# One transformer block on one core: side work of the vector engine moved between units, chunks paced wider, five low parts split over two engines

## The chip, the cores and the metric

The kernel runs on one core of a Trainium2 chip. The core has a matrix engine (TensorE, PE in the profile, with its weight loads as PEld), a vector engine (VectorE, DVE), an activation engine (ScalarE, ACT), a general engine (GpSimd, POOL) and a queue that issues the transfers (SyncE, SP). Each runs its own instructions in order; semaphores order them among each other. The metric is the time of one execution on the device, in microseconds (us). The kernel before takes 740.03 us, the median of 3 runs (738.38 to 742.38).

## The reference

The block has a modulation vector, attention with a sliding window, and a feed-forward layer with Mish, for S = 2048 tokens of width D = 448, 16 heads of width 28, a window of 256 and F = 1792:

```python
mod = (_silu(c) @ w_mod).reshape(c.shape[0], 6, 1, -1)
sa, ca, ga, sb, cb, gb = (mod[:, 0], mod[:, 1], mod[:, 2], mod[:, 3], mod[:, 4], mod[:, 5])
h = _layernorm(x, axis=-1) * (1 + ca) + sa
x = x + ga * _A_ref(h, A_wqkv, A_wo)
h = _layernorm(x, axis=-1) * (1 + cb) + sb
x = x + gb * _B_ref(h, B_w1, B_b1, B_w2)
```

`_A_ref` projects to q, k and v, takes scores q k / sqrt(28), masks all but the last 256 keys of each query, takes the softmax and the sum over v, and projects with `wo`. `_B_ref` is `mish(h @ w1 + b1) @ w2`. All of it is in 32-bit floats. The kernel reaches that with rounded operands of 32 bits (F32R): each operand is a high part and a low part (what rounding left), and a product is high x high + high x low + low x high.

## The kernel before, in words

The tokens are four groups of 512 (`NG`, `GT`), and the attention works on one group and one head at a time: 64 pairs, each in three **units**, so 192 units (`NU`), written out by one loop over `u` (L920 before). A unit holds one block of keys for one head. Its number within the head is k = u mod 3.

What a unit writes out:
- `PV(u-3, Pl)`: the sum over v with the low parts of the probabilities of three units ago (L639).
- `B(u)`: scores with keys on the partitions, into one of two banks `sB` (L608, masks by L619), and two exponentials by ACT, the plain one `P` (L622) and the rounded one `Ph` (L623).
- `SP(u-1)`: POOL subtracts, `Pl = P - Ph` (L629): the low part. Three buffers each of `P`, `Ph` and `Pl`.
- `A(i, t)`: scores of a head three heads ahead, with queries on the partitions, into one of two banks `sA` (L578), and DVE's maximum of each query over its keys (L580). Four of these belong to a head, so k = 0 and k = 2 have one and **k = 1 has two** (`A(a, 1)` and, at the end of the unit, `A(a, 2)`). Every second head `M2` (L586) transposes the maxima, and DVE splits them (L588, L589); a transfer puts them under the queries.
- `E`, `E2`, `E3`: the division by the sum of probabilities for two heads at once; its reciprocal and a sum are DVE's (L663, L664, at k = 1), its product POOL's (L666).
- `PV(u-2, Ph)`: the sum over v with the high parts. There is one bank `pv`; ACT copies it out (L644).

Between these stands other work for PE. Each group has a **filler** (`fill_main`): a generator that writes out the projections to q, k and v of the same and the next group (`gen_qkv`, L294), the transposes of the normalised tokens into four chunks of channels (`gen_hT`, L232), the transposes of attention's output (`gen_oT`) and the output projection (`gen_wo`). Each unit gets a credit of `RATE[g]`, and filler steps are taken while the credit is above zero; a step costs what it yields, or `RATE[g]` where it yields nothing. Two banks `mm` hold all filler. What a filler step leaves for ACT (high part) and DVE (low part) is put into `pipe` and comes out at the start of the next units (`pipe.step()`): for a chunk the high part (L239) one unit on and the low part (L236, L243) two units on.

Next to it each group has a **side** generator (`fill_side`), one step a unit (`side_step`): the first normalisation of the next group (`gen_ln1`: statistics L192 and L193, then L222 for each of four tiles, each followed by POOL's copy of 64 columns, L196), the sums of the modulation (`gen_wm_sum`, DVE, L145 and L147), and in group 3 the first pieces of the feed-forward weights (`gen_w1`, split by L164 on ACT and L170 or L172 on DVE). A side generator that yields the word "bank" is not stepped while the pipe holds a bank. What is left of a group's generators when the next group begins is written out at once (`drain`).

Transfers are written to SP's queue in the order of `dma` calls (L59); those in `later` are taken out one at a time by the loop, or all at once by `flush`. `load_slot` loads queries and keys of a head five heads ahead of the unit, from a scratch tensor `scr` to which the projections went.

After the loop comes the feed-forward stage (L813, L989 to L991), which the change does not touch.

## Time and profile before

| what | value |
|---|---|
| median of 3 runs | 740.03 us (738.38 to 742.38) |
| the profiled execution, whole | 743.38 us |
| its span, first to last instruction | 741.6 us |
| PE busy in the span | 695.8 us |
| mean granted clock of PE | 0.982 |
| units 0 to 191 | 56.4 to 434.5 us |

In the profile's rows an engine's name and the kernel's line come first, then the operation, what it writes and reads, and the shapes. "[1.02 <-DVE hl L243]" means that the engine was idle for 1.02 us before, and that the instruction of DVE that writes `hl` ended this. A row of waits gives the waiting engine, what it waited for, the total in us, how often, and the longest. A row of a stretch gives its start and end, its length, the busy time (and number of instructions) of PE, PEld, DVE, ACT and POOL, then PE's clock, the share of the transfer engines and GB/s. Units are not marked in the trace; unit u begins where the first score matmul (L608) of its block stands.

### The profile page before, as it was taken

The page shows a single profiled execution, that of the slowest core. Times are in us where ns is not written, and L with a number is a line of the kernel's source. Part 1 is how long each engine was busy: PE and PEld are TensorE (multiplying, and loading weights), DVE is VectorE, ACT ScalarE, POOL GpSimd, SP SyncE. Part 2 cuts the span into 40 slices and gives each one's busy share as a digit, 9 for nine tenths or more (in the row PEclk, how much of TensorE's full clock was granted, in tenths as well). Part 3 has the DMA queues.
Part 4 walks back from the last instruction along what each step waited for, and adds up shares of the span by engine and source line. Part 5 has one row for each costly group of instructions (what it writes and reads, how often), then busy time and mean ns, then how long its engine had stood idle before and what let it go on. Part 6 is the DMA issues. An engine that isn't in the chain of part 4 may idle for free.

```text
span 741.6 us, 11907 instructions
## 1 busy us (share of the span) xinstructions
PE 695.8 (94%) x3969; PEld 591.2 (80%) x3969; DVE 378.9 (51%) x1009; ACT 392.8 (53%) x740; POOL 331.4 (45%) x358
## 2 busy tenths in 40 slices
PE   3988989999999999999999889999999999999996
PEld 2866768778789888888887768878888888888885
DVE  4768546596765587665567843342323232413113
ACT  4416767676766677667778883343223222322221
POOL 4714788586666586666778854522010000000000
PEclk9898989999999999999999999999999999999999
DMA  8766644355274364453476155500200020001001
GB/s 211 204 226 221 166 139 129 94 178 179 86 226 154 100 221 144 133 179 92 145 215 204 50 187 164 145 24 1 100 0 1 1 99 1 1 0 50 1 0 50
DMA packets 48121, 83.86 MB, mean 113 GB/s; under 512 B 6126, under 2 KB 26108, under 8 KB 48060
## 3 DMA queue, kind: packets, MB, share of 16 engines
q1 hardware_dynamic: 48060, 83.10, 37.0%
q8 instruction: 32, 0.52, 0.3%
q14 instruction: 29, 0.24, 0.1%
HBM read 53.45 MB, written 29.36 MB: 112 GB/s over the span
## 4 chain that ended last, share of the span: by engine, by line
PE 77%; DVE 9%; DMA 7%; issue 3%; ACT 2%; POOL 1%; SPq 1%; DVEq 0%; POOLq 0%; ACTq 0%
PE z L813 19%; PE pv L639 9%; PE qk L294 6%; PE acc L990 6%; PE acc L991 6%; PE acc L989 6%; PE qk_v L294 5%; PE sA L578 4%; PE wo L294 4%; PE sB L608 4%; DMA k<-scr 3%; PE sB L619 3%; DVE junk L580 3%; PE et L650 1%; PE qk L401 1%
## 5 line engine op out<-in xcount | busy, mean ns | idle before, releaser
L629 POOL TENSOR_TENSOR Pl<-P,Ph 128x512 fp32r<-128x512 f32 (+2 forms) x192 | 236.7, 1240 | 94.0 <-ACT Ph L623 53.4
L580 DVE CUSTOM_DVE_ANT_0 junk<-sA,mask 128x384 f32<-128x384 f32 (+2 forms) x256 | 134.9, 527 | 116.7 <-PE sA L578 112.7
L622 ACT ACTIVATE P<-sB 128x512 f32<-128x512 f32 (+2 forms) x192 | 109.9, 572 | 65.0 <-PE sB L619 62.7
L821 DVE TENSOR_TENSOR al<-t,ah 128x512 fp32r<-128x512 f32 x56 | 38.8, 692 | 204.9 <-ACT ah L820 204.9
L819 ACT ACTIVATE t<-z,b1c 128x512 f32<-128x512 f32 x56 | 38.6, 689 | 193.3 <-PE z L813 182.4
L578 PE MATMUL sA<-k,q 84*128 84x384 f32 (+2 forms) x256 | 102.3, 403 | 10.7 <-DVE mx L580 6.0
L623 ACT ACTIVATE Ph<-sB 128x512 fp32r<-128x512 f32 (+2 forms) x192 | 109.3, 569 | 0.0
L813 PE MATMUL z<-hhf,w 128*128 128x512 f32 x224 | 89.4, 399 | 0.0
L813 PE MATMUL z<-hlf,w 128*128 128x512 f32 x224 | 88.7, 396 | 0.0
L989 PE MATMUL acc<-w2h,ah 128*128 128x448 f32 x224 | 82.2, 367 | 0.0
L990 PE MATMUL acc<-w2l,ah 128*128 128x448 f32 x224 | 82.0, 366 | 0.0
L991 PE MATMUL acc<-w2h,al 128*128 128x448 f32 x224 | 81.9, 366 | 0.0
L639 PE MATMUL pv<-Ph,v 128*60 128x256 f32 (+2 forms) x352 | 77.6, 294 | 3.0 <-ACT o L644 2.5
L639 PE MATMUL pv<-Pl,v 128*60 128x256 f32 (+2 forms) x352 | 74.5, 286 | 2.2 <-POOL Pl L629 2.1
L608 PE MATMUL sB<-q,k 86*128 86x256 f32 (+1 forms) x352 | 75.2, 288 | 1.0 <-DMA q<-mr 1.0
L813 PE MATMUL z<-hhf,w1l 128*128 128x512 f32 x168 | 66.4, 395 | 0.0
L608 PEld LDWEIGHTS sB<-q,k 86*128 86x128 f32 x352 | 62.6, 192 | 2.6 <-issue 1.0
L578 PEld LDWEIGHTS sA<-k,q 84*128 84x128 f32 x256 | 50.3, 197 | 16.8 <-DVE mx L580 10.1
L619 PE MATMUL sB<-fdmask,identr 128*128 128x128 bf16 (+1 forms) x320 | 60.9, 256 | 0.0
L639 PEld LDWEIGHTS pv<-Ph,v 128*60 128x60 f32 x352 | 45.5, 134 | 19.0 <-ACT o L644 6.0
L639 PEld LDWEIGHTS pv<-Pl,v 128*60 128x60 f32 x352 | 45.5, 133 | 11.8 <-POOL Pl L629 4.8
L644 ACT ACTIVATE o<-pv 60x512 f32<-60x512 f32 x64 | 37.8, 591 | 30.3 <-PE pv L639 29.8
(148 smaller groups left out, 1257.5 us busy)
## 6 DMA issues: line engine op xcount, KB each, us to landing
scr<-st SPq DMA_DIRECT2D x24, 512.0 KB
k<-scr SPq DMA_DIRECT2D x48, 252.0 KB
q<-scr SPq DMA_DIRECT2D x64, 168.0 KB
scr<-st SPq DMA_DIRECT2D x32, 256.0 KB
x<-x1d SPq DMA_DIRECT2D x10, 448.0 KB
xin<-in_A_x_dram SPq DMA_DIRECT2D x8, 448.0 KB
xr<-in_A_x_dram SPq DMA_DIRECT2D x16, 224.0 KB
x1d<-xr SPq DMA_DIRECT2D x16, 224.0 KB
```

What stands on the lines that cost most here:

```text
L294: PE.matmul(p, b, a, start=(n == 0), stop=(n == 10))
L578: PE.matmul(p[:, c0:384], q[0:84, t * 128:(t + 1) * 128], k[0:84, t * 128 + c0:t * 128 + 384], start=True, stop=True)
L580: DVE.tensor_tensor_reduce(out=junk[:, c0:384], in0=p[:, c0:384], in1=mask[:, c0:384], scale=1.0, scalar=-3.0e38, op0=ALU.add, op1=ALU.max ...
L608: PE.matmul(p[:, c:c + 128 * (t1 - t0)], k[:, jj * 128:(jj + 1) * 128], q[:, t0 * 128:t1 * 128], start=(n == 0), stop=False, skip_group_ch ...
L622: ACT.activation(P[:, c0:], p[:, c0:], AF.Exp, scale=SCALE)
L623: ACT.activation(Ph[u][:, c0:], p[:, c0:], AF.Exp, scale=SCALE)
L629: POOL.tensor_tensor(Pl[u][:, c0:], Pt[u][:, c0:], Ph[u][:, c0:].bitcast(F32), op=ALU.subtract)
L639: PE.matmul(pv[0:60, t0 * 128:t1 * 128], V[j % NV][:, h, :], P[u][:, c:c + 128 * (t1 - t0)], start=(P is Ph and b == 0 and n == 0), stop=F ...
L813: PE.matmul(zb[n], ps[m][1], ps[m][0], start=(m == 0), stop=(m == 10))
L989: PE.matmul(p, ah[n][:, ts], w2h[f], start=(f == 0), stop=False)
L990: PE.matmul(p, ah[n][:, ts], w2l[f], start=False, stop=False)
L991: PE.matmul(p, al[n][:, ts], w2h[f], start=False, stop=(f == NF - 1))
```

## The change

```diff
@@ gen_ln1
         for r in gen_ln([xin[g][:, t, 0:D] for t in range(4)], qk, xn_tiles, f"a{g}", act):
             if r:
                 XS[g] = r
-            yield 0.4
+            yield "dve"
@@ gen_hT
             pipe.add(2, lambda p=p, ci=ci: hT_hi(p, ci, hh, 0), lambda p=p, ci=ci: hT_lo(p, ci, hh, hl, 0))
-            yield
+            yield 1.2
@@ gen_wm_sum
         for k in range(4):
+            yield "dve"
             mod_sum(k, ws[k], ws[0])
-            yield
         yield
@@ SP
-        POOL.tensor_tensor(Pl[u][:, c0:], Pt[u][:, c0:], Ph[u][:, c0:].bitcast(F32), op=ALU.subtract)
+        for eng, a, b in ((POOL, c0, 512),) if u < NU - 5 else ((POOL, 0, 256), (DVE, 256, 512)):
+            eng.tensor_tensor(Pl[u][:, a:b], Pt[u][:, a:b], Ph[u][:, a:b].bitcast(F32), op=ALU.subtract)
@@ gen_w1
             w1_hi(n)
-            yield
+            yield "dve"
             w1_lo(n, DVE)
@@ gen_ln2
             xs = r or xs
-            yield 0.35
+            yield 0.6
@@
-    def side_step(g):
-        if told.get(g) != "bank" or not pipe.held():
+
+    def side_step(g, two):
+        if not (told.get(g) == "bank" and pipe.held() or told.get(g) == "dve" and two):
             told[g] = next(side[g], None)
-    RATE = {0: 0.48, 1: 0.88, 2: 0.88, 3: 0.62}
+    RATE = {0: 0.48, 1: 0.91, 2: 0.91, 3: 0.65}
@@ the loop over units
             if v > 1:
-                side_step(g)
+                side_step(g, k == 1 and a < NS)
```

(Before the loop the call becomes `side_step(0, False)`.) A side generator that has yielded the word "dve" is not stepped in a unit with two maxima, so the work after that yield is written out one unit later there. A chunk costs 1.2 of credit; before, it cost the group's rate. The last normalisation, which in group 3 is filler, costs 0.6 a step instead of 0.35. Groups 1 to 3 get 0.03 more credit a unit. In units 187 to 191 the low part of the probabilities is made by POOL for columns 0 to 255 and by DVE for columns 256 to 511; for the others POOL makes all of it. No operation is added or removed, but for those five, which become two each.

How instructions move, at three places. First DVE in group 1, from the reciprocal of unit 55 on, before (`xin` are the tokens of group 2 being normalised, `hlo` the low part of attention's output of group 0, `junk` the maxima; the row after each maximum, which reads its result, is left out but for the first):

```order
L663 RECIPROCAL rc_2014<-et_1955 128x8
L664 TENSOR_TENSOR ol_1994<-ol_1994,et_1955 128x224
L222 TENSOR_SCALAR xin_758<-xin_758,mva_1859,rsa_1967 128x448
L580 ISA junk,mx_1880<-sA_2_2030,mask 128x384
L580 ISA mx_1880 128x1
L511 TENSOR_TENSOR hlo_2020<-ot_2021,hho_2019 128x512
L580 ISA junk,mx_1880<-sA_3_2050,mask 128x384
```

and now:

```order
L664 RECIPROCAL rc_2014<-et_1952 128x8
L665 TENSOR_TENSOR ol_1988<-ol_1988,et_1952 128x224
L580 ISA junk,mx_1885<-sA_2_2029,mask 128x384
L580 ISA mx_1885 128x1
L511 TENSOR_TENSOR hlo_2020<-ot_2021,hho_2019 128x512
L580 ISA junk,mx_1885<-sA_3_2049,mask 128x384
```

The normalisation of a tile no longer stands between the two maxima of unit 55; the four of them come in units 57, 59, 60 and 62 instead of 55, 56, 57 and 58.

Second, SP in group 0, from the write of the query maxima of heads 6 and 7 (`mr`) to the loads of heads 10 and 11 (`wop` are pieces of the output weights, `st` projections of group 1), before:

```order
L59 DMA q_0_350<-mr_988 1x8x128 x2
L59 DMA wop_967<-in_A_wo_dram 64x448 x2
L59 DMA scr<-st_3_936 64x2x512
L59 DMA scr<-st_3_936 64x512
L59 DMA q_2_352<-scr 84x512
L59 DMA k_4_361<-scr 84x512
L59 DMA k_5_363<-scr 84x512
```

and now, from the write of the maxima of heads 4 and 5 on (`xin` are the tokens of group 2):

```order
L59 DMA q_2_352<-mr_812 1x8x128 x2
L59 DMA xin_834<-in_A_x_dram 128x2x448 x2
L59 DMA q_1_351<-scr 84x512
L59 DMA k_2_357<-scr 84x512
L59 DMA k_3_359<-scr 84x512
L59 DMA q_0_350<-mr_967 1x8x128 x2
L59 DMA wop_947<-in_A_wo_dram 128x448
L59 DMA scr<-st_0_892 128x2x512
L59 DMA scr<-st_0_892 128x512
L59 DMA wop_974<-in_A_wo_dram 128x448
L59 DMA q_2_352<-scr 84x512
L59 DMA k_4_361<-scr 84x512
```

(A second store of each shape and the second load of the same queries' buffer are left out.) The tokens of group 2 were loaded ahead of the maxima of heads 4 and 5 before; now they come behind them, and other pieces and stores stand ahead of the load of head 10 (`q_2`, `k_4`).

Third, DVE in the last units of group 3 (`wm` are sums of the modulation, `trf` and `hlf` chunks of the feed-forward's input), before:

```order
L147 SCALAR_TENSOR_TENSOR wm5_0_5716<-wm5_1_5742,sT_132,wm5_0_5716 112x448
L147 SCALAR_TENSOR_TENSOR wm5_0_5716<-wm5_2_5772,sT_132,wm5_0_5716 112x448
L236 TENSOR_SCALAR trf03_5897<-trf03_5897,cols_131 128x512
L243 TENSOR_TENSOR hlf0_5736<-trf03_5897,hhf0_5735 128x512
L147 SCALAR_TENSOR_TENSOR wm5_0_5716<-wm5_3_5802,sT_132,wm5_0_5716 112x448
L663 RECIPROCAL rc29_5963<-et29_5920 128x8
L664 TENSOR_TENSOR ol29_5944<-ol29_5944,et29_5920 128x224
L783 TENSOR_TENSOR w2l0_6061<-w2p0_5946,w2h0_6060 128x448
```

and now:

```order
L664 RECIPROCAL rc29_5958<-et29_5912 128x8
L665 TENSOR_TENSOR ol29_5939<-ol29_5939,et29_5912 128x224
L147 SCALAR_TENSOR_TENSOR wm5_0_5768<-wm5_1_5792,sT_132,wm5_0_5768 112x448
L630 TENSOR_TENSOR Pl187_5979<-P187_5952,Ph187_5953 128x256
L147 SCALAR_TENSOR_TENSOR wm5_0_5768<-wm5_2_5822,sT_132,wm5_0_5768 112x448
L630 TENSOR_TENSOR Pl188_5999<-P188_5975,Ph188_5976 128x256
L147 SCALAR_TENSOR_TENSOR wm5_0_5768<-wm5_3_5847,sT_132,wm5_0_5768 112x448
L630 TENSOR_TENSOR Pl189_6017<-P189_5995,Ph189_5996 128x256
L630 TENSOR_TENSOR Pl190_6036<-P190_6013,Ph190_6014 128x256
L630 TENSOR_TENSOR Pl191_6053<-P191_6032,Ph191_6033 128x256
L784 TENSOR_TENSOR w2l0_6066<-w2p0_5962,w2h0_6065 128x448
```

The three summations moved behind the reciprocal and the sum for heads 58 and 59, and DVE's five halves stand among them and behind them.

More of the change, by code (lines that the diff above doesn't have):

```diff
@@ L912, in adaln_block @@
                 flush()
-            side_step(0)
+            side_step(0, False)
         if i % 2:
```

## The prediction

> **What bounds the kernel now.** I read the page first, then the busy time of each engine by stage, then the waits of TensorE (PE), then timelines at the places where PE waits.
>
> ```profile
> span 741.6 us, 11907 instructions
> PE 695.8 (94%) x3969; PEld 591.2 (80%) x3969; DVE 378.9 (51%) x1009; ACT 392.8 (53%) x740; POOL 331.4 (45%) x358
> ```
>
> The profiled execution took 743.38 us (1.8 us around the span); the median of the runs shown is 740.03, so 3.35 is subtracted at the end. PE is the bound nearly everywhere, and the change leaves its matmuls as they are. A gain can only come out of PE's idle time, or out of stretches at a lower clock. By stage (up to the heads' loop, heads of the four token groups, the rest):
>
> ```profile
> 56.40:139.80 83.40, 75.08 (x468) 60.47 (x468) 50.93 (x177) 58.59 (x134) 59.40 (x61) 0.92 0.53 155
> 139.80:243.20 103.40, 99.68 (x676) 86.29 (x676) 68.69 (x213) 72.38 (x140) 69.29 (x64) 1.00 0.52 161
> 243.20:345.60 102.40, 99.58 (x679) 86.45 (x678) 69.33 (x214) 72.27 (x140) 69.80 (x64) 1.00 0.48 149
> 345.60:434.50 88.90, 82.61 (x576) 69.26 (x575) 61.02 (x174) 70.37 (x139) 69.98 (x63) 0.98 0.47 142
> ```
>
> Columns: length; busy us (instructions) of PE, weight loads, DVE, ACT, POOL; PE clock; DMA share; GB/s. Length less PE's busy time: 8.3, 3.7, 2.8 and 6.3 us idle, 21.1 in all. That, and the clock under 1.00 in groups 0 and 3, is all that can be won. Who ended the waits, in the whole program:
>
> ```profile
> PE sA L578 <- DVE mx L580: 6.0, 10, 1.0
> PE sA L578 <- DMA k<-scr: 4.5, 4, 2.8
> PE tr L232 <- DVE hl L243: 4.2, 4, 1.1
> ```
>
> Some 10 us wait for VectorE (DVE): for a score bank that its maximum has not freed (sA), or for a transposed chunk that it has not split (tr). The change aims at these.
>
> **Groups 1 and 2, normalisation among the output projection (units 55 to 59 and 103 to 107).** The place in group 1, first as a whole:
>
> ```profile
> 156.04:166.68 10.64, 9.40 (x72) 7.95 (x71) 10.54 (x29) 9.06 (x19) 10.58 (x14) 1.00 0.67 218
> 157.70 1.50 DVE L222 TENSOR_SCALAR xin<-xin,mva,rsa 128x448 f32<-128x448 f32 x1
> 157.76 0.45 PE L639 MATMUL pv<-Pl,v 128*60 128x128 f32 x2 [0.16 <-POOL Pl L629]
> 160.67 0.89 DVE L222 TENSOR_SCALAR xin<-xin,mva,rsa 128x448 f32<-128x448 f32 x1
> 160.80 0.27 PE L586 MATMUL mt<-ident,mx 128*8 128x128 f32 x1 [0.41 <-DVE mx L580]
> 164.57 0.50 DVE L222 TENSOR_SCALAR xin<-xin,mva,rsa 128x448 f32<-128x448 f32 x1
> 164.69 0.45 PE L578 MATMUL sA<-k,q 84*128 84x384 f32 x1 [0.67 <-DVE mx L580]
> ```
>
> DVE is busy 10.54 of 10.64 us here. In the new order the four normalisations stand in units 57, 59, 60 and 62, not in 55 to 58, so these four units lose 1.50 + 0.89 + 2 x 0.50 (the third is like the fourth) = 3.4 us of DVE and get one back (0.5 to 0.9): some 2.6 net, more than PE's three waits (0.16 + 0.41 + 0.67 = 1.24). But POOL is busy 10.58 of the 10.64 us: once DVE is early, POOL is next. It too loses work (three of the four 64-column copies behind each normalisation), about 1 us. I take 0.9 of the 1.24, twice: **1.8 us** (between 0 and 2.5).
>
> **Groups 1 and 2, transposed chunks (units 69 to 74).**
>
> ```profile
> PE qk L294 <- DVE hl L243: 0.4, 1, 0.4
> 189.54 0.82 DVE L236 TENSOR_SCALAR tr<-tr,cols 128x512 f32<-128x512 f32 x1
> 190.39 0.69 DVE L243 TENSOR_TENSOR hl<-tr,hh 128x512 fp32r<-128x512 f32 x1
> 191.23 0.63 PE L232 MATMUL tr<-ident,xin 128*128 128x128 f32 x4 [1.02 <-DVE hl L243]
> ```
>
> A chunk's split costs DVE 0.82 + 0.69 = 1.5 us, and two banks hold chunks, so the third waits for the first one's split. At 1.2 a chunk against a rate of 0.91 the first three still stand in consecutive units (69, 70, 71, as before); only the fourth moves on by one. The 1.02 us therefore shrinks only by what DVE is less late: a residual sum and its statistics, ahead of the split before, now stand one unit earlier. I put that at 0.3 of the 1.02, and 0.3 of the 0.4: 0.6, twice: **1.2 us** (0 to 2.8, if both waits went).
>
> **Group 0.** The raised rates (0.03 x 48 units = 1.4) pay in groups 1 and 2 for the dearer chunks (4 x 0.32 = 1.3) and in group 3 for the dearer normalisation (6 x 0.25 = 1.5), so filler ends there where it ended. Group 0 has no raise: here the chunks take 1.2 against a rate of 0.48, which is two or three units each, and all later filler slips. Counting the rows of the new PE order, 9 to 11 matmuls of 512 columns are behind from unit 6 to unit 42, and units 43 to 47, which had no filler, take them.
>
> ```profile
> 56.40:75.10 18.70, 16.16 (x92) 12.97 (x93) 15.28 (x39) 12.49 (x27) 9.47 (x9) 0.82 0.70 222
> 86.78 1.39 SPq L59 DMA_DIRECT2D q<-mr  x2
> 82.97:94.22 11.25, 10.42 (x70) 8.47 (x70) 6.63 (x26) 8.59 (x20) 9.30 (x11) 1.00 0.80 191
> 97.54 0.44 PE L578 MATMUL sA<-k,q 84*128 84x128 f32 x1 [2.85 <-DMA k<-scr]
> 132.90:139.85 6.95, 6.08 (x44) 4.51 (x42) 5.42 (x21) 5.99 (x16) 5.21 (x6) 1.00 0.21 62
> ```
>
> Start: DVE is busy 15.28 of 18.70 us and sets the pace; up to unit 13 it has the same work in both orders, so removing PE's two chunk waits mostly turns them into waits for maxima: 0.3 won. End: 6.95 - 6.08 = 0.87 us of idle takes the slipped matmuls: 0.9. Middle: head 10's load is behind the write of query maxima (86.78), two pieces of the output weights and four stores, and lands at 97.54, 2.85 us late. In the new SP order it has one weight piece, two stores and another piece ahead: by their shapes 224 + 768 + 224 KB instead of 224 + 768. With its own 336 KB that is 1.55 MB after the query maxima; at the 191 GB/s of the row above 8.1 us, after the 1.39 of their issue: 9.5, where it was 97.54 - 86.78 = 10.8. The 896 KB of x now stand two loads ahead of the query maxima; if they are not through, 4.7 us at the same rate come on top. I take 1.1 won (from 3 lost, part of that delay, to 2.85 won).
>
> The clock adds to this:
>
> ```profile
> 93.12:96.53 3.41, 1.57 (x12) 1.04 (x10) 1.06 (x3) 2.90 (x6) 3.41 (x5) 1.00 0.85 220
> 96.53:103.36 6.83, 5.82 (x23) 4.88 (x24) 1.83 (x9) 1.57 (x4) 4.24 (x5) 0.50 0.46 152
> 103.36:110.20 6.84, 6.58 (x46) 5.31 (x44) 4.09 (x17) 5.88 (x15) 5.95 (x7) 1.00 0.33 99
> 407.15:410.56 3.41, 2.07 (x14) 1.39 (x12) 3.23 (x12) 1.99 (x5) 3.41 (x4) 1.00 0.00 0
> 410.56:413.97 3.41, 3.39 (x15) 2.78 (x16) 2.33 (x7) 2.29 (x4) 3.41 (x5) 0.50 0.39 119
> 427.63:431.04 3.41, 2.17 (x13) 1.39 (x14) 1.40 (x4) 2.91 (x6) 2.04 (x4) 1.00 0.53 140
> ```
>
> Stretches at half clock begin whole multiples of 3.41 us apart, each after a stretch of 3.41 us with PE busy 1.57 or 2.07; one with 2.17 was not followed by one. The one at 96.53 ran 23 matmuls in 6.83 us where the next 6.84 ran 46: less the 1.0 idle inside, 6.83 - 1.0 - 23 x 6.84/46 = 2.4 us lost. It goes if the load's wait drops below some 1.3 us (3.41 - 2.1); I give that two chances in five: 1.0. Group 0: 0.3 + 0.9 + 1.1 + 1.0 = **3.3 us** (3 lost to 7 won). The Trainium skill, page "TensorE: Matmul & The Clock Gate", section "Part 1: The HAM clock gate", has the clock halve after an idle window of about 3.4 us; here it halved after windows with only 1.3 to 1.8 us idle, so the measurement decides. By the page no wait here would cost clock, and the sum below would be 1.4 us smaller.
>
> **Group 3, units 170 to 180.** The input weights' low parts and the last normalisation leave the units with two maxima, or come one at a time.
>
> ```profile
> 398.19 0.60 DVE L170 TENSOR_TENSOR w1l<-w1p,w 128x448 fp32r<-128x448 f32 x1
> 402.14 1.28 POOL L629 TENSOR_TENSOR Pl<-P,Ph 128x512 fp32r<-128x512 f32 x1 [0.61 <-POOL Pl L629]
> 402.19 1.72 DVE L170 TENSOR_TENSOR w1l<-w1p,w 128x448 fp32r<-128x448 f32 x1
> PE sA L578 <- DVE mx L580: 1.8, 2, 1.0
> 398.39:416.15 17.76, 15.15 (x101) 12.15 (x100) 15.77 (x40) 13.23 (x26) 16.06 (x16) 0.90 0.43 134
> ```
>
> 1.8 us wait for maxima. POOL is busy 16.06 of 17.76, with the same work after, so at most 1.7 can go; I take 1.0. The half clock at 410.56 costs 15 matmuls' progress where 14 ran in a stretch with 1.3 idle; at the 46 per 6.84 us above, 3.41 - 15 x 0.149 = 1.2 us; a third of that, 0.4. **1.4 us** (1 lost to 2.9 won).
>
> **The last five low parts.** POOL takes columns 0 to 255, DVE the others.
>
> ```profile
> L629 POOL TENSOR_TENSOR Pl<-P,Ph 128x256 fp32r<-128x256 f32 x16 | 12.2, 761 | 1.7 <-PE sA L578 0.9 <-ACT Ph L623 0.8
> PE pv L639 <- POOL Pl L629: 1.3, 3, 0.9
> 416.15:434.50 18.35, 14.81 (x111) 11.56 (x110) 11.73 (x24) 16.67 (x34) 15.10 (x13) 1.00 0.19 52
> ```
>
> A POOL half costs 0.76 us against 1.28 whole (402.14). DVE's half is not in the trace: from 448 columns in 0.60, an estimated 0.35. But the two engines do not overlap on such operands: the same 0.60 became 1.72 at 402.19, ending 0.48 after POOL's instruction ended. So a pair costs 0.76 + 0.35 = 1.1, one after the other, not 0.76: 0.2 won of each 1.28. And DVE's halves stand behind the three summations of the modulation (448 columns, same kind of operands), which now come exactly here, at up to 1.7 us each when they meet POOL; in their place the reciprocal and sum before POOL's product come ahead of them, which frees POOL sooner. Of the 1.3 us that PE waits for low parts I take **0.5** (1.3 won to 3 lost); ACT, busy 16.67 of 18.35, allows no more than 1.7 in this stretch anyway. Each half waits on DVE for ACT's rounded copy; behind it stand the next summation and half and then the first low parts of the feed-forward, for which PE waits after 437 us. The Trainium skill, page "SBUF — State Buffer", section "SBUF: two separate sides", says that DVE with two SBUF inputs and POOL reading SBUF take a shared port pair in turn, whole instructions at a time: it speaks against this split, and the 1.72 agrees. Without it the term would be 1.3.
>
> **Sum.** 1.8 + 1.2 + 3.3 + 1.4 + 0.5 = 8.2. The profiled 743.4 becomes 735.2; the median 740.0 becomes 731.8.
>
> **Rivals.**
> 1. POOL sets the pace where DVE did (its 10.58 of 10.64 and 16.06 of 17.76 speak for it; against it, that PE's waits there name DVE). Groups 1 to 3 keep only the chunks' 1.2, and group 0 loses its clock term: 1.2 + 2.3 = 3.5 won, 736.5.
> 2. DVE stays late: no work leaves it, the pieces only meet other units, and the order shows a normalisation of the last kind still between two maxima in unit 175, since its pace of 0.6 is a filler's cost and no mark for such units. Against it: DVE is busy only 68.7 of 103.4 us in group 1. Only the 0.9 + 1.1 of group 0 remain: 738.
> 3. All of it works: PE's waits at all these places go and both late half-clock stretches too. 8.3 + 3.7 + 2.8 + 1.8 + 1.3 = 17.9 of idle and 2.4 + 1.2 of clock; two thirds of that, since each place keeps its next limit, 14.3: 726.
>
> ```profile
> 56.40:82.97 26.57, 23.45 (x137) 18.49 (x137) 20.17 (x57) 17.47 (x39) 14.36 (x14) 0.87 0.65 199
> ```
>
> 4. Slower: the clock gate at the start. With filler held back, PE has 6.08/5 = 1.2 us of work a unit (units 43 to 47, without filler) where DVE needs 15.28/10 = 1.5 (units 0 to 9): busy 0.8; at 2.07 of 3.41 (0.61) the clock halves. From that share on it decides. If every stretch from 56 to 80 us falls below that, the first 14 units (137 matmuls in 26.57 us before, 127 then) run at 23 in 5.8 us: 32.0, 5.4 more, with 10 matmuls (2.3 us) still to do, and the last units, at 0.64 now, gate once as well (2.4). 10.1 lost against 8.2 - 0.3 - 1.0 - 0.5 = 6.4 won: 744.
>
> **Chances.** Forecast 0.50 (728 to 736); POOL's pace 0.18; DVE stays late 0.12; all of it 0.12; the gate 0.08. The range 726 to 740 leaves out the gate's case, half of the best one and the forecast's edges, about 2 in 10. A measurement of this kernel can tell about 0.5%, 3.7 us: faster means below 736.3, slower above 743.7. Faster: nearly all of the forecast and the best case, and half of rival 1: 0.70. Slower: 0.07. Within: 0.23.
>
> **What would show it.** Units 55 to 59: DVE's busy share falls and the waits for L580 go; if POOL then ends PE's waits, rival 1. The third chunk's wait for L243 stays, at 0.7 or so, in both groups. The wait for k<-scr near unit 21 is below 2 us, and whether a half-clock stretch follows settles the clock term. PE idle from unit 43 to 47 is gone. DVE's 256-column low parts show 0.35 us alone and about 1.1 where POOL is reading. The forecast is wrong if PE's idle time in the four groups stays above 16 us.

## The result

The changed kernel takes 735.41 us, the median of 7 runs (733.93 to 736.76), beside 742.38 us of the kernel before in its 7 runs there (738.38 to 745.53). The ratio is 0.9907, with a 95% interval of 0.9883 to 0.9931: faster by 0.9%. The profiled execution took 735.41 us where the one of before took 743.38: 8.0 us less, where the prediction's sum was 8.2. The time lies inside the predicted range (726 to 740). The forecast itself, 731.8, was 3.6 us too low, and 2.3 of these come from its base: the kernel before has a median of 742.38 in seven runs, where the three runs known then had 740.03. The parts of the sum are another matter.

First the profile page of the changed kernel, span and busy time:

```profile
span 733.6 us, 11903 instructions
PE 692.8 (94%) x3969; PEld 589.6 (80%) x3969; DVE 383.1 (52%) x1014; ACT 392.0 (53%) x740; POOL 326.5 (45%) x358
```

Then its four groups, the same stretches as in the prediction (length; busy us of PE, PEld, DVE, ACT, POOL; PE clock; transfers):

```profile
58.28:137.42 79.14, 71.55 (x468) 57.69 (x469) 49.83 (x176) 58.25 (x133) 58.77 (x61) 0.98 0.55 164
137.42:239.04 101.62, 99.62 (x677) 86.42 (x676) 70.96 (x215) 72.44 (x141) 68.62 (x63) 1.00 0.53 162
239.04:341.00 101.96, 99.88 (x679) 86.65 (x679) 70.98 (x215) 72.12 (x140) 68.58 (x63) 1.00 0.50 149
341.00:426.05 85.05, 80.47 (x572) 67.80 (x572) 62.33 (x178) 69.35 (x137) 68.87 (x63) 1.00 0.48 145
```

Length less PE's busy time is 7.6, 2.0, 2.1 and 4.6 us: 16.3 of idle time, where it was 21.1. The groups became shorter by 4.3, 1.8, 0.4 and 3.9 us. Against that the part ahead of unit 0 took 1.9 us more (58.28 for 56.37), and what follows the last unit is 0.5 us longer. In group 0 the idle time fell by 0.7 only; its mean clock rose from 0.92 to 0.98. And the waits of PE in the whole program (in total, times, longest):

```profile
PE sA L578 <- DVE mx L580: 5.4, 13, 0.9
PE sA L578 <- DMA k<-scr: 3.8, 2, 3.0
PE pv L640 <- POOL Pl L630: 3.0, 8, 0.6
PE tr L232 <- DVE hl L243: 1.6, 2, 0.8
```

Waits for the split of a chunk (`hl`) fell from 4.2 to 1.6, those for maxima from 6.0 to 5.4 only, and those for POOL's low parts rose from 2.1 to 3.0. Of the 3.8 us for loads 0.7 stand ahead of unit 0, so 3.1 are in group 0.

### The profile page after: what moved, and what is told of

Same layout as the page of the kernel before. It is cut to its first block, busy times and chain, and to the rows that moved or that the text cites. A ratio compares the mean times of both kernels' runs of the same rounds, so it can differ in the third digit from the quotient of the medians.

```text
span 733.6 us, 11903 instructions
## 1 busy us (share of the span) xinstructions
PE 692.8 (94%) x3969; PEld 589.6 (80%) x3969; DVE 383.1 (52%) x1014; ACT 392.0 (53%) x740; POOL 326.5 (45%) x358
## 4 chain that ended last, share of the span: by engine, by line
PE 75%; DVE 9%; DMA 6%; ACT 4%; SPq 2%; issue 2%; POOL 1%; DVEq 0%; POOLq 0%; ACTq 0%
PE z L814 20%; PE pv L640 8%; PE qk L294 7%; PE acc L992 6%; PE acc L993 6%; PE acc L991 6%; PE sA L578 5%; PE wo L294 4%; PE sB L608 4%; PE qk_v L294 3%; PE sB L619 3%; DVE junk L580 3%; SPq L59 2%; PE et L651 1%; ACT P L622 1%
## 5 line engine op out<-in xcount | busy, mean ns | idle before, releaser
L630 POOL TENSOR_TENSOR Pl<-P,Ph 128x512 fp32r<-128x512 f32 (+2 forms) x192 | 232.9, 1221 | 84.4 <-ACT Ph L623 50.9
L578 PE MATMUL sA<-k,q 84*128 84x384 f32 (+2 forms) x256 | 100.8, 397 | 9.7 <-DVE mx L580 5.4
L640 PE MATMUL pv<-Ph,v 128*60 128x256 f32 (+2 forms) x352 | 76.8, 292 | 2.2 <-ACT o L645 2.1
L578 PEld LDWEIGHTS sA<-k,q 84*128 84x128 f32 x256 | 49.0, 193 | 18.0 <-DVE mx L580 11.5
```

What stands on the lines that cost most here:

```text
L578: PE.matmul(p[:, c0:384], q[0:84, t * 128:(t + 1) * 128], k[0:84, t * 128 + c0:t * 128 + 384], start=True, stop=True)
L630: eng.tensor_tensor(Pl[u][:, a:b], Pt[u][:, a:b], Ph[u][:, a:b].bitcast(F32), op=ALU.subtract)
L640: PE.matmul(pv[0:60, t0 * 128:t1 * 128], V[j % NV][:, h, :], P[u][:, c:c + 128 * (t1 - t0)], start=(P is Ph and b == 0 and n == 0), stop=F ...
```

## The experiments

Each kernel is told apart from the one named beside it by a few lines. Ratios are to the kernel before, run beside it on the same chip. In rows of c2_defer, d2_norm_late and e1_chunk_two line numbers are two higher than in the changed kernel, where those after L629 are one higher than before. "Start" is the time of unit 0; "group 0" is the time from there to the first score matmul of unit 47, "group 3 and rest" from that of unit 143 to the end, both in the one profiled execution.

| kernel | median us | ratio (95%) | start | group 0 | group 3 and rest |
|---|---|---|---|---|---|
| before, two profiles | 742.1 to 744.0 | 1 | 56.4, 57.0 | 82.0, 81.8 | 398.1, 396.5 |
| changed | 735.4 | 0.9907 (0.9883 to 0.9931) | 58.3 | 77.6 | 394.1 |
| a1_no_split | 736.5 | 0.9910 (0.9877 to 0.9943) | 56.5 | 77.0 | 394.7 |
| a2_no_mark | 735.4 | 0.9892 (0.9860 to 0.9924) | 58.1 | 75.9 | 397.8 |
| a3_no_chunk | 736.0 | 0.9903 (0.9872 to 0.9934) | 56.0 | 77.8 | 397.4 |
| a4_no_ln2 | 738.7 | 0.9925 (0.9896 to 0.9953) | 55.8 | 75.8 | 398.1 |
| c3_g3_only | 740.8 | 0.9974 (0.9954 to 0.9993) | 56.3 | 77.5 | 397.1 |
| c1_mark_g3 | 731.9 | 0.9849 (0.9819 to 0.9879) | 56.3 | 75.2 | 395.3 |
| c2_defer | 735.5 | 0.9903 (0.9869 to 0.9936) | 58.9 | 77.1 | 393.8 |
| d1_x_late | 732.1 | 0.9865 (0.9835 to 0.9895) | 56.5 | 75.3 | 393.9 |
| d2_norm_late | 731.1 | 0.9841 (0.9817 to 0.9865) | 57.4 | 75.2 | 394.3 |
| d3_chunk_g12 | 736.7 | 0.9913 (0.9879 to 0.9948) | 58.1 | 78.5 | 396.7 |
| e1_chunk_two | 730.7 | 0.9846 (0.9817 to 0.9874) | 56.6 | 75.6 | 395.4 |

The start differs by 3 us between kernels whose programs are the same there; it belongs to no kernel. The columns of stretches come from one execution each, so a difference of a microsecond between two of them counts only where several kernels show it.

**One part undone at a time.** First the last five low parts, whole and on POOL again:

```diff
-        for eng, a, b in ((POOL, c0, 512),) if u < NU - 5 else ((POOL, 0, 256), (DVE, 256, 512)):
+        for eng, a, b in ((POOL, c0, 512),):
```

> The changed kernel with one part undone: the last five low parts of probabilities are whole again and on POOL alone. The changed kernel stands at 0.9907 of the kernel before. Theory (the prediction's term, 0.5 us for this part): 0.9914, with PE's waits for low parts in the last units some 0.5 us longer. Rival (an overlap of the two engines saves what a half saves, 0.5 of each 1.3 us): 2 us or more are lost, 0.9935. Second rival (the two halves run one after the other and DVE's own queue is longer, so the split gains nothing): 0.9907 or below, and PE's idle time from unit 182 on is not larger than in the changed kernel.

Measured: 0.9910, which the interval does not tell from the changed kernel, nor from the theory's 0.9914 or the rival's 0.9935. The place itself is told by the trace. Units 182 to 191 of the changed kernel and of this one:

```profile
410.60:424.02 13.42, 10.99 (x84) 8.56 (x84) 12.58 (x25) 12.58 (x25) 12.46 (x12) 1.00 0.16 43
```

```profile
407.86:422.28 14.42, 11.21 (x84) 8.57 (x84) 12.06 (x23) 13.35 (x26) 13.44 (x12) 1.00 0.19 51
```

The split is worth 1.0 us in these two profiles, between the theory's 0.5 and the first rival's 2. DVE's halves in the changed kernel, all five and two of them, with the summation between:

```profile
L630 DVE TENSOR_TENSOR Pl<-P,Ph 128x256 fp32r<-128x256 f32 x5 | 2.6, 526 | 1.4 <-ACT Ph L623 0.9 <-issue 0.4
420.96 0.41 DVE L630 TENSOR_TENSOR Pl<-P,Ph 128x256 fp32r<-128x256 f32 x1
421.29 0.98 DVE L147 SCALAR_TENSOR_TENSOR wm<-wm,sT,wm 112x448 f32<-112x448 f32 x1
421.75 4.26 POOL L630 TENSOR_TENSOR Pl<-P,Ph 128x256 fp32r<-128x256 f32 x4
422.19 0.94 DVE L630 TENSOR_TENSOR Pl<-P,Ph 128x256 fp32r<-128x256 f32 x1
```

The half at 420.96 took 0.41 us (0.35 was estimated), and so, within 0.03, did three of the others; the one that started behind POOL's first took 0.94 (1.1 was estimated). None of the five ran wholly with POOL at rest: four of POOL's halves beside DVE's work took 4.26 us, 1.07 each, where 0.76 was read before the change and a whole takes 1.28. The Trainium skill, page "SBUF — State Buffer", section "SBUF: two separate sides", has the two engines take turns on such operands; 0.94 for 0.41 and 1.07 for 0.76 agree with it.

Second, the marks (the word "dve", which keeps side work out of units with two maxima) ignored, so that side work is issued in every unit:

```diff
-                side_step(g, k == 1 and a < NS)
+                side_step(g, False)
```

> The changed kernel with one part undone: side work is issued in every unit again, also in units with two maxima. Theory (the prediction: 0.9 us in each of groups 1 and 2, and about 1.0 in group 3 from the input weights' low parts): 2.8 us lost, 0.9945, and the waits of PE for maxima in units 55 to 59 and 103 to 107 are back at about 1.1 us a group. Rival (POOL sets the pace there: PE waits for POOL's low parts now for 0.67 us in units 55 to 59, so the wait only changed its releaser): 1 us lost or less, 0.9907 to 0.9920, PE's idle time in units 55 to 59 within 0.5 us of the changed kernel's 0.75.

Measured: 0.9892, no loss at all; the theory's 0.9945 is outside the interval. In units 55 to 59 PE waits 1.0 us for maxima here:

```profile
PE sA L578 <- DVE mx L580: 0.7, 1, 0.7
PE mt L586 <- DVE mx L580: 0.3, 1, 0.3
```

In the changed kernel these are gone, and in the same units stands

```profile
PE pv L640 <- POOL Pl L630: 0.7, 2, 0.4
```

So the rival holds at this place: the wait changed its releaser, and some 0.25 us of it went. But the table says more: "group 3 and rest" is 3.7 us longer without the marks (397.8 for 394.1; 0.8 of it is a late write of maxima, told in the last section), and group 0 is shorter (75.9). The marks gain in group 3 and lose elsewhere.

Third, the pace of the chunks and the rates of groups 1 and 2 as before:

```diff
-            yield 1.2
+            yield
-    RATE = {0: 0.48, 1: 0.91, 2: 0.91, 3: 0.65}
+    RATE = {0: 0.48, 1: 0.88, 2: 0.88, 3: 0.65}
```

> The changed kernel with one part undone: transposed chunks are paced as before in all groups, with the rates of groups 1 and 2 as before. Theory (the prediction: 3.3 us in group 0 and 0.6 in each of groups 1 and 2 hang on the pace of the chunks): 4.5 us lost, 0.9968; the idle time of PE in units 42 to 47 is back at about 1 us and that of the third and fourth chunk of a group at 1.5 us. Rival (group 0's gain is the clock, which goes by where the wait for the load of head 10 falls, and that wait stayed at 3 us in the changed kernel): half-clock stretches of 6.8 us come back as in the kernel before or not at all, and without them the loss is 2 us or less, 0.9934 or below.

Measured: 0.9903, the same as the changed kernel. The chunks' waits are back (1.5 us in units 69 to 73 and again in 117 to 121), and yet nothing is lost in the end. The theory's 0.9968 falls. With the marks in all groups the pace of the chunks buys nothing that the whole program shows (its profile has 204.65 us for 203.57 in units 48 to 143, and half clock after the last unit); without them it does (d3_chunk_g12, below). Half clock came back in group 0, 11.0 us of PE's busy time for 3.4, and still group 0 took 77.8 us for 77.6.

Fourth, the last normalisation at 0.35 a step and group 3's rate at 0.62:

```diff
-            yield 0.6
+            yield 0.35
-    RATE = {0: 0.48, 1: 0.91, 2: 0.91, 3: 0.65}
+    RATE = {0: 0.48, 1: 0.91, 2: 0.91, 3: 0.62}
```

> The changed kernel with one part undone: the last normalisation's steps cost 0.35 again and group 3's rate is 0.62. Theory (the last normalisation is not what holds PE in units 173 to 182; the input weights' low parts are): within 0.5 us of the changed kernel, 0.9900 to 0.9914. Rival (the normalisation and these low parts meet in the same units, and spreading it is most of group 3's gain): 1 us or more lost, 0.9920 or above, and PE waits for maxima in units 173 to 180 by 1 us more than in the changed kernel (0.7).

Measured: 0.9925, 3.3 us above the changed kernel in the medians, as the rival has it; the two intervals overlap, so the place has to decide. Units 170 to 181, in the order before (second profile), changed, without the marks, without this pace:

```profile
395.00:416.44 21.44, 18.75 (x135) 15.17 (x134) 18.59 (x53) 17.54 (x35) 19.86 (x20) 1.00 0.50 153
```

```profile
391.02:410.60 19.58, 17.82 (x133) 14.73 (x132) 17.78 (x50) 17.66 (x36) 18.67 (x20) 1.00 0.49 155
```

```profile
388.64:410.08 21.44, 18.90 (x132) 14.77 (x132) 18.78 (x50) 17.73 (x36) 19.60 (x20) 1.00 0.47 148
```

```profile
386.35:408.47 22.12, 18.86 (x135) 15.09 (x134) 18.93 (x53) 18.36 (x36) 20.07 (x20) 1.00 0.46 141
```

The two parts together win 1.9 us here. The pace alone wins 0.8 at most (0.84 of the 21.44 us are a late write of maxima, told in the last section) and the marks alone nothing; in all of "group 3 and rest" each alone is no shorter than before (397.8 and 398.1, against 396.5). The reading that fits, and was not tested further, is the rival's: the normalisation and the weights' low parts meet in the same units, and moving one of them only lets it meet the other somewhere else.

**The kernel before, profiled again.**

> The kernel before, profiled a second time, to see which parts of its first profile repeat. In the first profile group 0 (units 0 to 47) lost 8.3 us to PE's idle time and half of 11.5 busy us to half clock. Theory (the half clock in group 0 belongs to the kernel before, since the stall at head 10's load and the early chunk waits are in its order): again over 9 us busy at half clock in group 0. Rival (where a half-clock stretch falls is chance, and the changed kernel's 3.4 us was luck): clearly fewer, below 6 us.

Its two stretches at half clock in group 0 came again:

```profile
59.62:66.45 6.83, 5.71 (x23) 4.67 (x24) 4.77 (x15) 3.52 (x6) 2.01 (x3) 0.50 0.71 229
97.16:103.99 6.83, 6.48 (x26) 5.54 (x27) 2.34 (x10) 2.23 (x6) 3.22 (x4) 0.50 0.48 151
```

PE was busy 12.2 us at half clock, 11.5 the first time; group 0 took 81.8 us, 82.0 the first time. So these stretches belong to the program of before, not to one execution; what they cost is another question, taken up with group 0's account below. The stretch of half clock in group 3 did not come again, so of the 4 us by which "group 3 and rest" became shorter 1.6 are not the change's (398.1 against 396.5).

**Group 3's part alone, on the kernel before.**

```diff
-            yield 0.35
+            yield 0.6
             w1_hi(n)
-            yield
+            yield "dve"
             w1_lo(n, DVE)
-                side_step(g)
+                side_step(g, k == 1 and a < NS and g == NG - 1)
-    RATE = {0: 0.48, 1: 0.88, 2: 0.88, 3: 0.62}
+    RATE = {0: 0.48, 1: 0.88, 2: 0.88, 3: 0.65}
```

The yields of the four summations in `gen_wm_sum` are those of the change too, which puts a summation one unit later in every group.

> The kernel before with the changes of group 3 alone: its side work kept out of units with two maxima and its last normalisation's steps at 0.6 with the rate at 0.65. Chunks, groups 0 to 2 and the last five low parts are as before. Theory (these two parts are needed together and carry 3.7 us, half of the whole gain): 0.9945 to 0.9955, PE's idle time in group 3 falls from 6.3 to about 5. Rival (prediction: this part is worth 1.4 us, most of the gain is in group 0): 0.998.

Measured: 0.9974, 1.9 us, near the rival. In its profile "group 3 and rest" did not gain at all (397.1). Two reasons can be named: the split low parts, 1.0 us, are not in it, and in unit 180 PE waited 1.28 us for a write of maxima, as in the next run. What this kernel did gain is group 0, 77.5 us for 82, although its program there differs from the one before only in that the four summations of units 5 to 9 stand one unit later on DVE. The wait for head 10's load was 1.67 us in place of 2.85 and 2.51, and no half clock followed it. Against that its units 48 to 143, where too only the summations moved, took 1.4 us more than before (207.05 for 205.7). The later summations are a part of the change too, and no run undid them alone: what they are worth in group 0 stays open.

**The marks in group 3 alone.** All else is the changed kernel.

```diff
-                side_step(g, k == 1 and a < NS)
+                side_step(g, k == 1 and a < NS and g == NG - 1)
```

> The changed kernel, with side work kept out of units with two maxima in group 3 alone; the wider chunks and the split low parts stay. Without these marks in any group the time was the changed kernel's, but its parts were not: in the profile of that run the stretch from unit 143 to the end took 3.7 us more, and group 0 some 1.7 us less (idle time plus half of the busy time at half clock, 7.6 against 9.3), with groups 1 and 2 the same. Theory (the marks are worth 3.7 us in group 3 and nothing in groups 0 to 2, where the wider chunks alone remove the same waits): 0.985 to 0.989 of the kernel before, 1 to 3 us better than the changed kernel. Rival (the difference in group 0 is which half-clock stretches happened to fall, and the marks are worth their predicted 0.9 us in each of groups 1 and 2): 0.9907 to 0.994.

Measured: 0.9849, below the changed kernel, and the intervals of the two do not overlap: a better kernel, by 3.5 us in the medians. The theory's sign is right; that the marks are worth nothing in groups 0 to 2 is not, since they cost time there. Group 0 takes 75.2 us, and the same program there takes 75.9 (a2_no_mark), 75.2 and 75.6 (d2 and e1, below); with the marks in group 0 it takes 77.6, 77.0 and 75.8 (changed, a1, a4): some 1.4 us more in the mean. The trace of the changed kernel shows where:

```profile
110.96 0.33 PE L640 MATMUL pv<-Pl,v 128*60 128x256 f32 x1 [0.35 <-POOL Pl L630]
112.23 1.15 POOL L172 TENSOR_TENSOR wo<-wop,wo 64x448 fp32r<-64x448 f32 x1
114.51 0.39 PE L640 MATMUL pv<-Pl,v 128*60 128x384 f32 x1 [0.62 <-POOL Pl L630]
```

The marks hold up the whole side generator of group 0, and with it POOL's work on the output weights, which now ends in unit 31 and not in unit 28. Two of these operations, 1.15 us each, stand ahead of low parts for which PE waits in units 30 and 32: the two units take 3.9 us where they take 2.5 here. The three profiles with the marks and the wider pace (changed, a1, a4) have these waits, and a3_no_chunk has such ones in units 31 and 33; no profile without the marks has any in units 30 to 33.

In groups 1 and 2 it is the normalisation (the changed kernel, then this one; eight of the twelve are in these groups):

```profile
L222 DVE TENSOR_SCALAR xin<-xin,mva,rsa 128x448 f32<-128x448 f32 x12 | 11.1, 929 | 0.8 <-POOL rsa L207 0.8
```

```profile
L222 DVE TENSOR_SCALAR xin<-xin,mva,rsa 128x448 f32<-128x448 f32 x12 | 8.6, 718 | 0.8 <-POOL rsa L207 0.8
```

Kept out of units with two maxima, a normalisation starts beside POOL's subtraction of low parts more often and becomes longer (929 ns for 718, and 732 before). Units 55 to 59 are as long either way (10.58 and 10.54 us). But the last of the four, 0.50 us here, takes 1.49 in the changed kernel, and then a maximum is late for PE two units on (the rows are of group 2):

```profile
272.65 1.49 DVE L222 TENSOR_SCALAR xin<-xin,mva,rsa 128x448 f32<-128x448 f32 x1
277.04 0.45 PE L578 MATMUL sA<-k,q 84*128 84x384 f32 x1 [0.20 <-DVE mx L580]
```

Units 65 and 113 take 2.77 us each in the changed kernel, and 2.31 here and before; the two groups together take 203.6 us for 202.9. These places explain 2.1 of the 3.5 us; another 1.1 is a shorter wait for head 10's load (1.98 us for 3.05), which differs as much among kernels with one program there (2.36 in a1, 1.95 in a4). In the whole program PE waits 3.0 us for POOL's low parts with the marks everywhere, and 0.8 here.

**What makes head 10 wait.** Two transfers of group 0 held back, the output weights to unit 24 and the input of group 2 by some 24 units (the expectation's 16 is a miscount; the loop sets `now["u"]` to u):

```diff
+        while now["u"] < 24:
+            yield
         for ci in range(4):
             t = stg(qk, f"wop{ci}")
...
-            pipe.add(0, None, None, lambda: later.append(lambda: x_load(g + 1)))
+            pipe.add(0, *[None] * (28 if g == 1 else 2), lambda: later.append(lambda: x_load(g + 1)))
```

> The changed kernel, with two transfers of group 0 issued later: the four pieces of the output weights (0.8 MB) not before unit 24, the input of group 2 (0.9 MB) some 16 units later. Nothing else is moved but the work on these pieces. Theory (the wait of 1.4 to 3.1 us for the load of head 10 in unit 21 is the volume ahead of it in the queues): the wait for k in units 21 to 27 falls below 0.5 us, 2 to 3 us less idle time in group 0, and with it the half-clock stretch after unit 21: 0.986 to 0.988. Rival (the load is late because its issue stands behind the write of the query maxima, which DVE ends late): the wait stays at 2 us or more and the time within 0.5 us of the changed kernel, 0.9907.

Measured: 0.9903, nothing won. The wait in unit 21 went from 3.05 us to nothing, as the theory has it. But in units 27 and 33 PE now waits for the next loads:

```profile
PE sA L580 <- DMA k<-scr: 4.1, 2, 2.2
102.32 0.30 PE L580 MATMUL sA<-k,q 84*128 84x128 f32 x1 [1.89 <-DMA k<-scr]
```

4.1 us, where the changed kernel has 3.1 in group 0. Then the input of group 2 alone, on c1_mark_g3, with the line of `pipe.add` only:

> The kernel with the marks in group 3 alone (0.9849), with one transfer moved: the input of group 2 (0.9 MB) is loaded some 24 units later, near unit 35; the output weights stay where they are. When both were held back, the 3.05 us wait of unit 21 went to nothing, but 1.9 and 2.2 us came back in units 27 and 33, where the held weights and stores stood ahead of the next loads. In nine profiles so far each wait of 1.95 us or more in unit 21 was followed by half clock, each of 1.67 or less was not, and units 21 to 24 then took 6.5 to 7.5 us beyond the wait against 4.5 to 5.0. Theory (the 0.9 MB ahead of head 10's load make the wait of 2.0 us there): the wait falls below 1 us, no half clock follows, 3 to 4 us won: 0.979 to 0.981. Rival (TensorE then only reaches the next loads sooner, which stand behind the next write of maxima and four stores): waits of about 2 us in units 27 or 33 take its place, 0.9835 to 0.986.

Measured: 0.9865, and the wait in unit 21 was what it was. The rows are of d1_x_late, the write of the maxima, the issue of head 10's keys and the matmul that waits for them:

```profile
82.07 1.46 SPq L59 DMA_DIRECT2D q<-mr  x2
86.92 0.61 SPq L59 DMA_DIRECT2D k<-scr  x1
91.81 0.30 PE L578 MATMUL sA<-k,q 84*128 84x128 f32 x1 [2.01 <-DMA k<-scr]
```

So neither theory nor rival: the 0.9 MB of the input are not what the load waits for. What c2_defer took away from before that load, and this run did not, are the output weights; no run held these back alone, so that they are the cause is argued and not shown. Why the waits then come in units 27 and 33 was not tried. The trace shows that the next loads stand on SP behind the next write of maxima and the stores, at a time that the maxima set.

**The normalisations held back by four units** in groups 1 and 2, behind the splits of attention's output, on c1_mark_g3:

```diff
+        for _ in range(4 if key in ("a2", "a3") else 0):
+            yield
         xs = xn_tiles()
```

> The kernel with the marks in group 3 alone (0.9849), with the four normalisations of the next group held back by four units in groups 1 and 2: units 59 to 62 in place of 55 to 59, behind the splits of the attention output. In its profile PE waits 1.05 us in each of units 55 to 59 and 103 to 107, where VectorE and GpSimd meet on these operands. Theory (it is this meeting that holds PE, not which unit has two maxima): the waits fall below 0.4 us in both groups and nothing of the kind appears in units 60 to 69; 1.2 us won, 0.983. Rival (the work is the same and the wait moves with it, as with the marks, where 0.2 us of idle time came back in units 65 and 113): within 0.5 us of 0.9849.

Measured: 0.9841. In units 55 to 59 of its profile no wait is left. The one of units 60 to 68 is for a load:

```profile
PE sA L580 <- DMA k<-scr: 0.6, 1, 0.6
```

In units 103 to 107 there is none either, and 0.2 us of idle time stand in units 108 to 116. Groups 1 and 2 take 201.6 us (units 48 to 144), 202.9 in c1_mark_g3: the 1.2 us of the theory, which the medians (731.1 and 731.9) are too coarse to show. What holds PE there is the meeting of four normalisations with four splits, and not the second maximum of a unit.

**The chunks of group 0 at the old pace,** those of groups 1 and 2 at the new one, on c1_mark_g3:

```diff
-            yield 1.2
+            yield 1.2 if g > 1 else None
```

> The kernel with the marks in group 3 alone (0.9849), with the chunks that are transposed during group 0 paced as before, those of groups 1 and 2 still at 1.2. It prices the wider pace in group 0 alone. Theory (prediction: 0.3 at the start and 0.9 at the end of group 0, no clock): 1.2 us lost, 0.9865. Rival (units 0 to 11, 21.1 us with the old pace and 17.2 with the new in the profiles, do not give that back later): 3 us or more lost, 0.989 or above. Second rival (the clock: with the old pace PE idles less at the start, so the half clock there falls on busy time): as the first in time, but with over 9 us busy at half clock in group 0 and less idle time than the 3.5 us of the kernel it is made from.

Measured: 0.9913, 4.8 us above c1_mark_g3 in the medians: the size of the first rival, not of the theory. The second does not hold, since PE was busy 6.5 us at half clock in group 0 and not over 9. Its six times stand in two clusters (733.4 to 734.8 and 738.7 to 739.8), so the size is uncertain. Group 0 takes 78.5 us; the same program takes 77.5 in c3_g3_only, and the new pace 75.2 to 75.9: 2.5 us on average. Of the rest of its profile's loss 1.8 us stand in the start, and 1.4 in "group 3 and rest", where one stretch of half clock fell after the last unit (the part behind unit 191 took 312.4 us for 309.7); the same happened in a3_no_chunk. So the wider pace in group 0 is worth some 2.5 us in group 0 when the marks are not there, and about 1 when they are (a3_no_chunk 77.8, against a mean of 76.8).

**Two units to each chunk in groups 1 and 2,** on d2_norm_late:

```diff
-            yield 1.2
+            yield 1.83 if g > 1 else 1.2
-    RATE = {0: 0.48, 1: 0.91, 2: 0.91, 3: 0.65}
+    RATE = {0: 0.48, 1: 0.96, 2: 0.96, 3: 0.65}
```

> The kernel with the marks in group 3 alone and the normalisations held back (0.9841), with each transposed chunk of groups 1 and 2 at a cost of 1.83, two units apart (units 68, 70, 72, 74 in place of 69, 70, 71, 73), and the rates of these groups at 0.96 so that filler ends where it ended. In every profile with the pace of 1.2, PE waits 0.8 us in unit 71 and again in unit 119 for the split of the first chunk. Theory (two banks and a split of 1.5 us on VectorE: a third chunk in consecutive units must wait, one unit more is enough): both waits go, 1.6 us won, 0.982. Rival (the work that slips fills units in which TensorE was already full, or VectorE, busy over half of these units, is late elsewhere): the waits go but the time stays within 0.5 us, 0.9835 to 0.985, with as much new idle time in units 74 to 95 and 122 to 143.

Measured: 0.9846, the rival. The third chunk's wait in the changed kernel, and then what stands in its place here:

```profile
188.47 0.63 PE L232 MATMUL tr<-ident,xin 128*128 128x128 f32 x4 [0.82 <-DVE hl L243]
```

```profile
182.87 0.44 PE L580 MATMUL sA<-k,q 84*128 84x384 f32 x1 [0.36 <-DVE mx L582]
188.36 0.44 PE L642 MATMUL pv<-Ph,v 128*60 128x128 f32 x2 [0.18 <-ACT o L647]
```

No chunk waits for a split any more. Half of the 0.82 is paid in maxima and copies, and groups 1 and 2 together are as long as in d2_norm_late (201.9 and 201.7 us from unit 47 to 143). The best kernel here is therefore d2_norm_late by its ratio and e1_chunk_two by its median, which no interval tells apart; both beat the changed kernel.

## Why the prediction was right, and where its steps were wrong

The time came out as forecast because errors of both signs cancelled; that is luck, and not the terms. By the rows of the result, group 0 won 4.3 us (forecast 3.3), groups 1 and 2 won 2.2 (3.0), group 3 with the last five low parts won 3.9 (1.9); the part ahead of unit 0 took 1.9 back and the end 0.5. By the prediction's own last criterion (idle time in the four groups above 16 us) it was narrowly wrong: 16.3.

- **Normalisation in groups 1 and 2, forecast 1.8 us.** PE's idle time in units 55 to 59 fell from 1.24 to 0.78 and in 103 to 107 from 1.20 to 0.74, and the first rival named what took the place of the waits: POOL's low parts. The lengths hardly moved (10.64 and 10.62 us, then 10.58 twice), and units 65 and 113 became 0.46 longer each. The step that failed is "I take 0.9 of the 1.24", and that the four units lose DVE time: the four operations of a group took 3.4 us before and 4.6 where they now stand. With the old pace of the chunks the marks do win 1.1 us in these groups (204.65 in a3_no_chunk for 205.7 before), with the wider pace they cost 0.7 (203.6 for 202.9 in c1_mark_g3).
- **Chunks in groups 1 and 2, forecast 1.2.** 1.55 and 1.54 us of idle time became 0.82 and 0.82, the wait of 0.4 for the first projection included: 1.45. The mechanism was right, with a residue of 0.8 where 0.7 was said. In the length of both groups the pace is worth 1.1 us beside the marks (203.57 for 204.65) and 2.0 to 2.9 without them (202.8 to 203.7 in a2_no_mark, c1_mark_g3, d1_x_late and d3_chunk_g12 for 205.7 before).
- **Group 0, forecast 3.3; measured 4.3.** The sum is near, but its terms are not. The start, forecast 0.3: units 0 to 13 took 26.6 us before (the prediction's row from 56.40 to 82.97), and now

```profile
58.28:80.33 22.05, 18.62 (x125) 14.61 (x126) 19.14 (x56) 16.24 (x37) 13.45 (x14) 1.00 0.62 198
```

  The waits for chunks did become waits for maxima, as said (3.1 us of idle time, then 3.4), and DVE has the same work but for one instruction. The step that failed is that DVE "sets the pace" there: it was busy 20.2 of 26.6 us before and is busy 19.1 of 22.05 now, so nearly the same work of DVE fits into 4.5 us less. PE has 12 matmuls fewer there (137, then 125). Units 14 to 47 hold these 12 and took 57.1 us for 56.8; the 0.9 us of idle time at their end is gone, as said. Head 10's load, forecast 1.1 won: the time from the maxima's write to PE's go was 10.8 us before, and is 10.8 now (83.70 to 94.48):

```profile
83.70 1.43 SPq L59 DMA_DIRECT2D q<-mr  x2
88.38 0.44 SPq L59 DMA_DIRECT2D k<-scr  x1
94.48 0.30 PE L578 MATMUL sA<-k,q 84*128 84x128 f32 x1 [3.05 <-DMA k<-scr]
```

  That step, 9.5 by bytes at 191 GB/s, failed; why the bytes take longer was not tried. **The clock, forecast 1.0:** PE was busy 5.71 + 5.82 us at half clock before (58.99 to 65.82 and 96.53 to 103.36) and 3.41 after. At head 10 the wait did not fall, and yet one stretch of half clock followed it and not two: units 21 to 23 took 6.5 us beyond the wait, 7.2 and 7.5 in the two profiles of before. That is 0.6 to 1.0 won, the right size by another way. At the start the half clock that is gone is not what won the time. a4_no_ln2 has the same program there, with half clock, and its units 0 to 13 took no longer:

```profile
55.77:77.69 21.92, 20.45 (x125) 16.63 (x126) 19.13 (x56) 16.75 (x37) 13.41 (x14) 0.87 0.61 199
```

  PE was busy 1.8 us longer and idle 2.0 us less. So half of the busy time at half clock must not be counted as lost where PE has idle time to spare.
- **Group 3, forecast 1.4, and the last five low parts, 0.5.** The two profiles of before put units 170 to 191 at 37.6 and 36.4 us; the changed kernel takes 33.0. Of these 3.4 to 4.6 us the split is 1.0, the pair of marks and pace 1.9, 0.5 is not told apart, and 1.2 is a stretch of half clock that the second profile of before did not have. Without the clock's share 1.0 + 0.5 were forecast and 3.4 measured, so both terms were too small. The step that failed is "with the same work after, at most 1.7 can go": POOL's busy time in units 170 to 181 fell too, from 19.86 to 18.67 us in the rows above, with the same 20 operations; that they met DVE's less is the likely reason, not a shown one. And the second rival's worry, that the normalisation's pace is no mark for units with two maxima, was no bar: without the pace the marks won nothing.
- **The rivals.** POOL's pace is true of units 55 to 59 and 103 to 107, and not of the whole. The slower case, a clock gate at the start, went the other way: the old pace had half clock in units 0 to 10 in 5 profiles of 5, the new one in 3 of 9. And where it fell there under the new pace it cost nothing that the lengths show: units 0 to 10 took 16.8 to 17.4 us with it and 16.5 to 17.5 without.
- **Not foreseen:** the 1.9 us ahead of unit 0, which no part of the change touches (a1 and a4, with the same program there, have 56.5 and 55.8 where the changed kernel has 58.3).

## What to carry to other kernels

Where two engines slow each other on the same kind of operands, keeping one engine's side work out of one crowded place only moves the meeting: look first at what the other engine runs in the place it goes to, and at what else the delayed queue of work carries with it (here POOL's output weights), and spread the two apart (here by four units, 1.2 us) before marking units. Parts that act on the same queue cannot be priced one by one: in group 3 the marks alone won nothing, the pace alone 0.8 us at most and both 1.9, and in groups 0 to 2 the marks took back part of what the chunks had won. Undo each part by itself once the whole is measured; the better kernel here was the change with half of one part left out.

## What the runs showed of the hardware

**Half clock after stretches that were far from idle.** The 3.41 us stretches around unit 21, and what followed. First the kernel before (second profile), the changed kernel and c1_mark_g3, where half clock followed:

```profile
93.75:97.16 3.41, 1.25 (x8) 0.72 (x6) 0.73 (x3) 2.46 (x6) 3.41 (x4) 1.00 0.78 220
```

```profile
92.41:95.82 3.41, 1.34 (x10) 1.18 (x11) 0.77 (x4) 0.26 (x1) 3.41 (x4) 1.00 0.81 176
95.82:99.23 3.41, 3.41 (x15) 2.85 (x15) 1.11 (x5) 1.62 (x4) 1.14 (x2) 0.50 0.34 71
```

```profile
89.34:92.76 3.42, 1.44 (x12) 1.10 (x12) 0.77 (x4) 1.57 (x4) 3.42 (x4) 1.00 0.37 115
```

And c3_g3_only, a2_no_mark and a3_no_chunk, where it did not:

```profile
93.12:96.53 3.41, 1.74 (x12) 1.20 (x11) 0.90 (x6) 2.40 (x6) 3.37 (x4) 1.00 0.60 179
```

```profile
90.70:94.12 3.42, 1.78 (x12) 1.24 (x11) 0.71 (x3) 2.62 (x6) 3.42 (x5) 1.00 0.47 146
```

```profile
92.42:95.83 3.41, 2.06 (x14) 1.46 (x12) 1.19 (x7) 2.38 (x5) 3.36 (x5) 1.00 0.93 269
```

In these rows PE busy 1.25 to 1.44 of 3.41 us was followed by half clock, 1.74 to 2.06 was not. It is no fixed share, though: elsewhere in the changed kernel 1.98 was followed by it and 1.93 was not:

```profile
48.03:51.45 3.42, 1.98 (x7) 1.09 (x8) 2.88 (x11) 0.60 (x1) 0.84 (x2) 1.00 0.30 115
420.09:423.50 3.41, 1.93 (x16) 1.53 (x16) 3.41 (x5) 3.05 (x6) 3.41 (x4) 1.00 0.31 77
```

By the wait for head 10 it reads so: 1.95 us or more was followed by half clock in eight profiles of eight, 1.68 or less in none of six. One stretch of it costs units 21 to 23, where PE has little idle time, some 1.6 us (they take 6.0 to 6.5 us beyond the wait, where it is 4.5 to 5.0 without), two cost some 2.5. Two followed in the two profiles of before, where PE still waited 1.0 and 0.4 us into the first (97.54 for 96.53, 97.51 for 97.16); one followed in the six where the wait ended ahead of it. What else decides stays open. The Trainium skill, page "TensorE: Matmul & The Clock Gate", section "Part 1: The HAM clock gate", asks for an idle window of about 3.4 us; none of these was idle, so the measurement decides.

**A write of maxima that lands late by chance.** In unit 180 of c1_mark_g3 PE waited for it, where the changed kernel, whose rows agree to 0.02 us over the 4 us up to there, did not:

```profile
403.83 0.47 PE L608 MATMUL sB<-q,k 86*128 86x384 f32 x2 [1.23 <-DMA q<-mr]
```

Three profiles of fourteen have this wait in unit 180 (0.84 to 1.28 us); it costs 1.3 us there, and it is part of why kernels with the same program differ.
